# Softcap attention, gated MLP and cosine MLP on one core: both halves' attention and gated MLP first, then both cosine MLPs

## The chip, the cores and the metric

The kernel runs on one core of one Trainium2 chip. The metric is the device time of one launch in microseconds (us), taken as the median of several runs. Five engines share the core's memory (SBUF): TensorE (PE, with its weight loads PEld) does the matrix products, VectorE (DVE), ScalarE (ACT) and GpSimd (POOL) the elementwise work, SyncE (SP) issues most transfers. Each engine runs its own list of instructions strictly in order; a wait of one instruction holds up all that stand behind it.

## The reference, cut to what matters

```python
# q, k, v: (4, 12, 448, 64) float32, cap = 30
s = q @ k.T / sqrt(64);  s = cap * tanh(s / cap)
p = exp(s - max(s));     attn = p / (sum(p) + 1e-9) @ v
x = attn laid out as (1792 tokens, 768)
# gated MLP, weights float64: 768 -> 1536 -> 768
y = (1 / (1 + exp(-(x @ w_gate))) * (x @ w_val)) @ w_out
# cosine MLP, weights float64: 768 -> 2048 -> 768
h = y @ w_in;  out = (h * cos(h)) @ w_out2
```

## The kernel before, in words

The 4 batches go in two halves (hf = 0, 1) of 2 batches, 896 tokens each. A half passes through attention (L402 to L454: scores `s`, transposes `t`, products `pv` and sums `den`), the gated MLP (`pg` and `pv` by `mm3`, L461, for 12 blocks of 128 columns; then `py` for 6 blocks) and the cosine MLP. That last one takes the 16 blocks of the hidden layer in groups of 6, 5 and 5: first `ph` of each block with `hidden()` behind it (L587 to L628), then the product `po` (L549) of the group with `w_out2`, in three column parts of 256, added into `acc`.

Each product is made of three: a value is kept as a high part (a cast) and a low part (the value less the high part), and high·high, high·low and low·high are summed. So every weight and every activation is split.

The weights arrive as float64 and are taken in 70 units, 36 of the gated MLP and 34 of the cosine MLP. A unit is a raw block of 768 KB. On the first use it is converted to float32 in place of other work: ACT takes Abs and Sign (L148, L150), DVE makes four passes (L164, L166, L170, L174), SP writes the result to a buffer `kept` in device memory (L194, 384 KB). `w_split` then makes the two parts: ACT the cast (L184), POOL the difference (L185), into one of seven `wts` buffers. In the second half the unit is loaded from `kept` into an `fpool` buffer and only split. The conversions are spread by hand: `w_step`, `w_front`, `w_back` and `w_early` (L205 to L240) stand at fixed places among the matrix work and carry the pipeline one unit on.

`hidden()` takes one block: ACT copies `ph` to `h` (L624) and makes `u` (L601), DVE rounds (`n` L602, `u` L603), ACT takes the sine (L608), DVE multiplies (L609), then `n` is split into `z` (ACT L612, POOL L613). `ph` lies in one of two PSUM buffers (`psS`), so the block after next can start only when `u` of this one has been made.

The stages stand in this order (L643 to L655): attention of half 0, gated and cosine MLP of half 0 (all 70 units converted there; ten steps of half 1's attention are issued beside the last group of its cosine MLP, `BESIDE`), the rest of half 1's attention, gated and cosine MLP of half 1.

Of the kernel before, what the change touches and what calls it, by code (L numbers as in the profile page):

```python
# [27 lines left out]
def softcap_attention_gated_mlp_cos_mlp(  # L28
# [32 lines left out]
    UK = 3  # L61
    UW = 768
    RAWB = 2
    FB = 3
    LAST = 2

    BESIDE = (8, 11, 14, 15, 16, 17, 18, 19, 20)


    PVS = ((), (), (0, 1, 2, 3), ())  # L70
# [10 lines left out]
    fpool = ctx.enter_context(tc.tile_pool(name="fpool", bufs=FB))  # L81
    wts = ctx.enter_context(tc.tile_pool(name="wts", bufs=7))
    tmp = ctx.enter_context(tc.tile_pool(name="tmp", bufs=4))
    small = ctx.enter_context(tc.tile_pool(name="small", bufs=7))
    psS = ctx.enter_context(tc.tile_pool(name="psS", bufs=2, space=PSUM))
    psA = ctx.enter_context(tc.tile_pool(name="psA", bufs=4, space=PSUM))

# [19 lines left out]
                for s in range(0, nf, UK):  # L107
                    yield cols(w_out2, f"wz_{g}_{nb}_{s}", f0 + s, min(UK, nf - s), nb * NB, NB)

    first_units = list(weight_units())  # L110
    NU = len(first_units)
    units = first_units * (B // BH)
    kept = [dram.tile([P, UW], F32, tag=f"kept{i}", name=f"kept{i}") for i in range(NU)]
    SPARE = (41, NU - 8)
    raw_t, f_t, w_t = {}, {}, {}
    pos = {"load": 0, "sign": 0, "conv": 0, "keep": 0, "split": 0, "use": 0}

    def f_tile(i):
        return fpool.tile([P, UW], F32, tag="f", name=f"f{i}")

    def w_load():
        i = pos["load"]
        pos["load"] += 1
        name, src, nk, n = units[i]
        if i >= NU:
            f_t[i] = f_tile(i)
            nc.sync.dma_start(out=f_t[i][:, : nk * n], in_=kept[i - NU][:, : nk * n])
            return
        if SPARE[0] <= i < SPARE[1] and i % 3 == 0:
            t = big_tile([P, UW, 2], I32, f"{name}_raw")[:, : nk * n]  # L130
        else:
            t = wts.tile([P, UW, 2], I32, tag="w", name=f"{name}_raw")[:, : nk * n]
        nc.sync.dma_start(out=t.rearrange("p (k f) t -> p k f t", k=nk), in_=src)
        raw_t[i] = t

    def w_sign():  # L140
        i = pos["sign"]
        pos["sign"] += 1
        if i >= NU:
            return
        _, _, nk, n = units[i]
        hi = raw_t[i][..., 1].bitcast(F32)
        f_t[i] = f_tile(i)
        nc.scalar.activation(out=f_t[i][:, : nk * n], in_=hi, func=AF.Abs)  # L148
        yield
        nc.scalar.activation(out=hi, in_=hi, func=AF.Sign, bias=tiny)  # L150

    def w_conv():
        i = pos["conv"]
        pos["conv"] += 1
        if i >= NU:
            yield
            yield
            return
        _, _, nk, n = units[i]
        raw = raw_t.pop(i)  # L160
        lo, hi = raw[..., 0], raw[..., 1]
        g = f_t[i][:, : nk * n]
        gi = g.bitcast(I32)
        nc.vector.tensor_scalar(out=g, in0=g, scalar1=F64_MIN_HI, scalar2=F64_MAX_HI, op0=ALU.max, op1=ALU.min)  # L164
        yield
        nc.vector.tensor_scalar(  # L166
            out=gi, in0=gi, scalar1=4, scalar2=REBIAS, op0=ALU.logical_shift_left, op1=ALU.bitwise_xor
        )
        yield
        nc.vector.scalar_tensor_tensor(  # L170
            out=gi, in0=lo, scalar=28, in1=gi, op0=ALU.logical_shift_right, op1=ALU.bitwise_or
        )
        yield
        nc.vector.scalar_tensor_tensor(  # L174
            out=gi, in0=gi, scalar=1, in1=hi, op0=ALU.logical_shift_right, op1=ALU.bitwise_xor
        )

    def w_split():
        i = pos["split"]
        pos["split"] += 1  # L180
        name, _, nk, n = units[i]
        r = f_t.pop(i)[:, : nk * n]
        t = wts.tile([P, 2, UW], F32R, tag="w", name=f"w{i}")[:, :, : nk * n]
        nc.scalar.copy(out=t[:, 0], in_=r)  # L184
        nc.gpsimd.tensor_tensor(out=t[:, 1], in0=r, in1=t[:, 0].bitcast(F32), op=ALU.subtract)  # L185
        w_t[i] = t.rearrange("p a (k f) -> p a k f", k=nk)

    def w_keep():

        i = pos["keep"]  # L190
        pos["keep"] += 1
        if i < NU:
            _, _, nk, n = units[i]
            nc.sync.dma_start(out=kept[i][:, : nk * n], in_=f_t[i][:, : nk * n])  # L194

    def w_loads():

        spare = SPARE[0] <= pos["load"] < SPARE[1]
        while pos["load"] < min(NU, pos["conv"] + RAWB + spare) or NU <= pos["load"] < min(len(units), pos["split"] + FB):
            w_load()  # L200

    def nothing():
# [199 lines left out]
    def attention(hf):  # L402


        lo, hi = hf * BH * NP, (hf + 1) * BH * NP
        mine = pairs[lo:hi]
        n = len(mine)
        a_load(*mine[0])
        a_load(*mine[1])
        a_load(*mine[2])  # L410
        a_load_v(*mine[0])
        yield
        a_prep(*mine[0], 0)
        a_prep(*mine[0], 1)
        yield
        a_prep(*mine[1], 0)
        a_prep(*mine[1], 1)
        yield
        for i in range(n + 1):
            if i + 3 < n:  # L420
                a_load(*mine[i + 3])
            if i + 1 < n:
                a_load_v(*mine[i + 1])
            for c in range(NC):
                if i < n:
                    a_scores(*mine[i], c)
                if i and c == 0:
                    a_exp(*mine[i - 1], 1)
                if i < n and c == 2:
                    a_exp(*mine[i], 0)  # L430
                if i and c == 2:
                    a_sum(*mine[i - 1])
                if i + 2 < n and c % 2 == 0:
                    a_prep(*mine[i + 2], c // 2)
                if 1 < i < n and c == NORM:
                    a_norm(*mine[i - 2])
                if i:
                    for cc in PVS[c]:
                        a_pv(*mine[i - 1], cc)
                if 1 < i < n and c == SPLIT:  # L440
                    a_split(*mine[i - 2], nc.gpsimd)
                if i >= n - 1 and c == 3:
                    a_norm(*mine[i - 1])
                if i == n and c == 0:
                    a_split(*mine[i - 2], nc.gpsimd)
                if hf == 0 and (i, c) in UNIT_LOADS:
                    w_load()
                if hf == 0 and (i, c) in UNIT_PIECES:
                    next(pieces, None)
                yield  # L450
        if hf == 0:
            for _ in pieces:
                pass
        a_split(*mine[n - 1], nc.vector)  # L454
# [17 lines left out]
    def tmp_tile(name):  # L472
        return tmp.tile([P, BH, S], F32, tag="tmp", name=name)

    def mlp(hf, before, beside):


        x = [x_t[i] for i in range(KD)]
# [1 line left out]
        for m in range(KF):  # L480
# [30 lines left out]
            g.append(gt)  # L511
            w_step()
            w_catch()
        y = []
        for m in range(KD):
            ps = ps_tile(f"py{hf}_{m}")
            for s in range(2):
                w = w_take()
                for kk in range(KF // 2):
                    i = s * KF // 2 + kk  # L520
                    mm3(ps, w, kk, g[i], i == 0, i == KF - 1)
                w_step()
            yt = big_tile([P, 2, BH, S], F32R, f"y{hf}_{m}")
            nc.scalar.copy(out=yt[:, 0], in_=ps[:, :, :S])
            nc.vector.tensor_tensor(out=yt[:, 1], in0=ps[:, :, :S], in1=yt[:, 0].bitcast(F32), op=ALU.subtract)
            y.append(yt)
        acc = {}
        for gi, (f0, nf) in enumerate(groups):
            last = gi == len(groups) - 1
            if last:  # L530
                next(beside, None)
            z = [hidden(hf, f, y, f0 + nf - 1 - f) for f in range(f0, f0 + nf)]
            z, more = [t for t, _ in z], z[-1][1]
            zf = [t.rearrange("p a c s -> p a (c s)") for t in z]
            for nb in range(DM // NB):
                ws = [w_take() for _ in range(0, nf, UK)]
# [22 lines left out]
                for t in range(NTT):  # L559
# [21 lines left out]
                        w_back()  # L581
                    if last:
                        store(hf, t, nb, acc[nb][:, t])
                        if nb * NTT + t in BESIDE:
                            next(beside, None)

    def hidden(hf, f, y, left):  # L587

# [54 lines left out]
    with tc.manual_schedule():  # L643
        nc.vector.memset(zeros, 0.0)
        nc.vector.reciprocal(out=tanh_scale, in_=cap_sb)
        nc.vector.tensor_scalar_mul(out=tanh_scale, in0=tanh_scale, scalar1=1.0 / float(D) ** 0.5)
        nc.scalar.activation(out=guard, in_=cap_sb, func=AF.Exp, scale=-1.0)
        nc.vector.tensor_scalar_mul(out=guard, in0=guard, scalar1=1e-9 / CP)
        att = [attention(hf) for hf in range(B // BH)] + [iter(())]
        steps = 3 + (BH * NP + 1) * NC - LAST  # L650
        for hf in range(B // BH):
            for i in range(steps):
                next(att[hf])
            mlp(hf, att[hf], att[hf + 1])
            steps -= 1 + len(BESIDE)  # L655


# [33 lines left out]
```

## Time and profile before

| what | value |
|---|---|
| median of 3 runs | 1256.31 us (1250.93, 1256.31, 1257.65) |
| profiled execution, its own time | 1251.45 us |
| its span | 1249.3 us |
| PE busy | 1213.8 us, 97% |
| DVE busy | 707.7 us, 57% |
| ACT busy | 589.5 us, 47% |
| POOL busy | 451.5 us, 36% |

The span is the profiled stretch inside the execution; 2.15 us of the execution's time lie around it. The stages of the profiled execution are: up to 379.2 us attention and gated MLP of half 0; to 652.56 us its cosine MLP with ten steps of the next attention; to 754.1 us the rest of that attention; to 1007.08 us the gated MLP of half 1 (`pg` and `pv` to 917.8 us, then `py`); to 1249.3 us its cosine MLP. A busy share over the whole span is a mean over these, so the stages are read one by one.

### The profile page before, as it was taken

To read this page: it belongs to the slowest core of one execution; us is meant where nothing else is said; L and a number is where in the kernel's file an instruction comes from. 1 tells how busy PE (TensorE), PEld (TensorE's weight loads), DVE (VectorE), ACT (ScalarE), POOL (GpSimd) and SP (SyncE) were. 2 spreads that over 40 slices of the span, in tenths; PEclk is the share of its full clock that TensorE was granted. 3 is DMA by queue.
4 is the path that set the end of the run, shared out by engine and by line. 5 is a ranking of instruction groups with operands and counts; after the bars stand their busy time and mean duration, and the time that the engine had idled before them with its cause. 6 is when DMAs were issued, how large, how long until landed. Compare 5 with 4: busy or idle time off the path is not lost.

```text
span 1249.3 us, 17220 instructions
## 1 busy us (share of the span) xinstructions
PE 1213.8 (97%) x7014; PEld 1046.7 (84%) x7014; DVE 707.7 (57%) x757; ACT 589.5 (47%) x673; POOL 451.5 (36%) x234
## 2 busy tenths in 40 slices
PE   8989999999999799999899999999999999999998
PEld 4445889999999799889885559999999999999998
DVE  6998688778775975998949971111110024024252
ACT  6885554455445565646548862222221135344150
POOL 3767133223232432424426753222232224235041
PEclk9999999999999899999999999999999999999999
DMA  7522456555562463256254201211122101213013
GB/s 163 142 65 86 155 190 189 169 173 172 175 193 93 138 203 111 84 180 180 85 166 105 68 1 51 59 56 51 51 63 61 58 23 51 65 44 93 14 43 98
DMA packets 124751, 130.17 MB, mean 104 GB/s; under 512 B 49792, under 2 KB 100608, under 8 KB 124672
## 3 DMA queue, kind: packets, MB, share of 16 engines
q1 hardware_dynamic: 124384, 129.00, 34.2%
q8 instruction: 55, 0.90, 0.3%
q14 instruction: 24, 0.20, 0.1%
q10 hardware_dynamic: 288, 0.07, 0.0%
HBM read 96.80 MB, written 32.24 MB: 103 GB/s over the span
## 4 chain that ended last, share of the span: by engine, by line
PE 76%; DVE 15%; issue 4%; ACT 3%; DMA 1%; SPq 1%; POOL 1%; DVEq 0%; POOLq 0%; ACTq 0%
PE po L549 16%; PE py L461 14%; PE pv L461 13%; PE pg L461 12%; PE ph L461 11%; PE pv L369 4%; DVE f L170 3%; PE s L340 3%; DVE f L174 3%; DVE r L388 2%; PE t L319 1%; PE den L385 1%; DVE f L166 1%; ACT p L343 1%; DVE f L164 1%
## 5 line engine op out<-in xcount | busy, mean ns | idle before, releaser
L185 POOL TENSOR_TENSOR w<-f,w 128x768 fp32r<-128x768 f32 (+1 forms) x140 | 268.5, 1922 | 692.1 <-ACT w L184 614.2
L549 PE MATMUL po<-w,z 128*128 128x256 f32 x1920 | 243.4, 287 | 15.8 <-ACT w L184 5.6
L549 PEld LDWEIGHTS po<-w,z 128*128 128x128 f32 x1920 | 237.4, 195 | 19.9 <-ACT w L184 5.8
L461 PE MATMUL ph<-y,w 128*128 128x448 f32 x1152 | 235.3, 366 | 0.0
L461 PEld LDWEIGHTS ph<-y,w 128*128 128x128 f32 x1152 | 216.1, 188 | 17.9
L461 PE MATMUL pv<-x,w 128*128 128x448 f32 x864 | 181.7, 367 | 1.0 <-DVE sg L507 1.0
L461 PE MATMUL pg<-x,w 128*128 128x448 f32 x864 | 181.5, 367 | 0.0
L461 PE MATMUL py<-g,w 128*128 128x448 f32 x864 | 177.2, 367 | 0.0
L461 PEld LDWEIGHTS pv<-x,w 128*128 128x128 f32 x864 | 161.9, 188 | 17.8 <-issue 3.1
L461 PEld LDWEIGHTS pg<-x,w 128*128 128x128 f32 x864 | 162.0, 188 | 16.4 <-issue 0.7
L461 PEld LDWEIGHTS py<-g,w 128*128 128x128 f32 x864 | 162.2, 188 | 14.6
L184 ACT CAST w<-f 128x768 fp32r<-128x768 f32 (+1 forms) x140 | 112.1, 809 | 35.4 <-DVE f L174 15.5
L343 ACT ACTIVATE p<-s,tanh_scale 112x896 f32<-112x896 f32 x96 | 93.0, 1010 | 42.1 <-PE s L340 42.0
L507 DVE TENSOR_TENSOR sg<-pv,sg 128x896 f32<-128x896 f32 x24 | 26.1, 1090 | 139.7 <-PE pv L461 139.7
L602 DVE TENSOR_SCALAR n<-u 128x896 f32<-128x896 f32 (+1 forms) x38 | 25.5, 671 | 120.5 <-ACT u L601 120.5
L349 ACT ACTIVATE p<-p,cap_sb 112x1792 f32<-112x1792 f32 x48 | 86.3, 1797 | 0.1
L509 ACT CAST g<-sg 128x896 fp32r<-128x896 f32 x24 | 22.6, 942 | 132.4 <-DVE sg L507 132.4
L369 PE MATMUL pv<-p,v 112*64 112x448 f32 x384 | 77.5, 545 | 2.7 <-PE t L319 2.7
L340 PEld LDWEIGHTS s<-st 64*112 64x112 f32 x576 | 45.7, 171 | 39.7 <-ACT p L343 19.0
L388 DVE RECIPROCAL r<-den 128x448 f32<-128x448 f32 x24 | 70.8, 2950 | 8.7 <-PE den L385 8.7
L340 PE MATMUL s<-st 64*112 64x448 f32 x576 | 73.2, 380 | 1.5 <-ACT p L343 1.4
L353 POOL TENSOR_TENSOR sum<-p 112x896 f32<-112x896 f32 x24 | 56.1, 2337 | 44.1 <-ACT p L349 26.0
(75 smaller groups left out, 1176.3 us busy)
## 6 DMA issues: line engine op xcount, KB each, us to landing
kept<-f SPq DMA_DIRECT2D x64, 384.0 KB, 2.8
f<-kept SPq DMA_DIRECT2D x64, 384.0 KB, 3.1
wi_raw<-in_moe_w_in_dram SPq DMA_DIRECT2D x16, 768.0 KB, 5.1
wg_raw<-in_moe_w_gate_dram SPq DMA_DIRECT2D x12, 768.0 KB, 5.1
wv_raw<-in_moe_w_val_dram SPq DMA_DIRECT2D x12, 768.0 KB, 4.9
wo_raw<-in_moe_w_out_dram SPq DMA_DIRECT2D x12, 768.0 KB, 4.7
wz_raw<-in_moe_w_out_dram SPq DMA_DIRECT2D x12, 768.0 KB, 5.2
q<-in_q_dram SPq DMA_DIRECT2D x48, 112.0 KB, 3.1
```

What stands on the lines that cost most here:

```text
L170: nc.vector.scalar_tensor_tensor(out=gi, in0=lo, scalar=28, in1=gi, op0=ALU.logical_shift_right, op1=ALU.bitwise_or)
L174: nc.vector.scalar_tensor_tensor(out=gi, in0=gi, scalar=1, in1=hi, op0=ALU.logical_shift_right, op1=ALU.bitwise_xor)
L184: nc.scalar.copy(out=t[:, 0], in_=r)
L185: nc.gpsimd.tensor_tensor(out=t[:, 1], in0=r, in1=t[:, 0].bitcast(F32), op=ALU.subtract)
L340: nc.tensor.matmul(ps[:CP, h, :S], lhsT=st[r, ki, ks], rhs=st[r, qi], start=(n == 0), stop=(n == 2))
L343: nc.scalar.activation(out=pt[:CP, j], in_=ps[:CP, :, :S], func=AF.Tanh, scale=tanh_scale[:CP])
L349: nc.scalar.activation(out=pt[:CP], in_=pt[:CP], func=AF.Exp, scale=cap_sb[:CP])
L353: nc.gpsimd.tensor_tensor(out=s, in0=pt[:CP, 1] if half == 0 else s, in1=pt[:CP, 0], op=ALU.add)
L369: nc.tensor.matmul(pv[h * D : (h + 1) * D, :S], lhsT=tv[:, h, c, :], rhs=pt[:CP, j, h, :], start=(c == 0), stop=(c == NC - 1),)
L388: nc.vector.reciprocal(out=r[:, 0], in_=den[:, :S])
L461: nc.tensor.matmul(ps[:, c, :S], lhsT=w[:, wi, kk, :], rhs=x[:, xi, c, :], start=(first and (wi, xi) == (0, 0)), stop=(last and (wi, xi) = ...
L549: nc.tensor.matmul(pos_t[t][:, :NB], lhsT=zf[kk][:, zi, t * P : (t + 1) * P], rhs=ws[kk // UK][:, wi, kk % UK, :], start=(kk == 0 and (zi, ...
```

## The change

The stages are put in another order: attention and gated MLP of half 0, the same of half 1, then the cosine MLP of half 1, and last that of half 0. `mlp` is parted into `mlp1` and `mlp2`. Between, `y` of half 0 waits in device memory (`ykept`), unsplit; `y_again` loads and splits it during the last group of half 1's cosine MLP.

The 34 units of the cosine MLP are no longer converted where they are first used. `background()` converts them one after the other, in pieces, three to a unit: Abs and Sign of the unit with the load of the next raw block (below: s); the first two DVE passes (c1); the last two and the write to `kept` (c2). Four pieces follow each of the 12 column blocks of the second gated MLP, four stand in each block of its `py`, two follow each hidden block of the cosine MLP of half 1 and five stand among the `po` of each of its groups, until all 103 are used. Both cosine MLPs load their units from `kept`. `fpool` gets a fourth buffer, with three units loaded ahead (`AHEAD`) as before. Nine steps of half 1's attention are issued beside `py` of half 0. A `small` buffer and the spare raw buffers go, and `v` of attention is loaded some pieces later.

```diff
-    FB = 3
+    FB = 4
+    AHEAD = 3
...
-    BESIDE = (8, 11, 14, 15, 16, 17, 18, 19, 20)
+    BESIDE = ((2, 10), (3, 2), (3, 6), (4, 1), (4, 5), (4, 8), (5, 1), (5, 5), (5, 8))
+    PIECES, BESIDE_Y, PIECES_H, BESIDE_O = 4, (2, 5, 8, 11), 2, (4, 8, 12, 16, 20)
+    AGAIN = (4, 6, 8, 10, 12, 14, 16)
...
-    small = ctx.enter_context(tc.tile_pool(name="small", bufs=7))
+    small = ctx.enter_context(tc.tile_pool(name="small", bufs=6))
...
+    N1 = 2 * KF + 2 * KD
+    seq = [*range(N1)] * 2 + [*range(N1, NU)] * 2
+    units = [unit[u] for u in seq]
...
-        if SPARE[0] <= i < SPARE[1] and i % 3 == 0:
-            t = big_tile([P, UW, 2], I32, f"{name}_raw")[:, : nk * n]
-        else:
-            t = wts.tile([P, UW, 2], I32, tag="w", name=f"{name}_raw")[:, : nk * n]
+        t = wts.tile([P, UW, 2], I32, tag="w", name=f"{name}_raw")[:, : nk * n]
...
+    def background():
+        raw = {N1: raw_tile(unit[N1])}
+        yield
+        for u in range(N1, NU):
+            _, _, nk, n = unit[u]
+            g = f_tile(f"b{u}")[:, : nk * n]
+            for _ in signs(raw[u], g):
+                pass
+            if u + 1 < NU:
+                raw[u + 1] = raw_tile(unit[u + 1])
+            yield
+            c = convert(raw.pop(u), g)
+            next(c)
+            next(c)
+            yield
+            for _ in c:
+                pass
+            nc.sync.dma_start(out=kept[u][:, : nk * n], in_=g)
+            there.add(u)
+            yield
...
-        while pos["load"] < min(NU, pos["conv"] + RAWB + spare) or NU <= pos["load"] < min(len(units), pos["split"] + FB):
+        while pos["load"] < min(N1, pos["conv"] + RAWB) or N1 <= pos["load"] < min(len(units), pos["split"] + AHEAD):
...
             for c in range(NC):
+                if i + 1 < n and c == 3:
+                    a_load_v(*mine[i + 1])
...
-    def mlp(hf, before, beside):
+    def mlp1(hf, before, beside):
...
             w_step()
             w_catch()
+            if hf:
+                for _ in range(PIECES):
+                    next(beside, None)
...
                     mm3(ps, w, kk, g[i], i == 0, i == KF - 1)
+                    if hf == 0 and (m, i) in BESIDE or hf and i in BESIDE_Y:
+                        next(beside, None)
                 w_step()
+            if hf == 0:
+                yt = tmp_tile(f"y{hf}_{m}")
+                nc.scalar.copy(out=yt, in_=ps[:, :, :S])
+                nc.sync.dma_start(out=ykept[m], in_=yt)
+                continue
...
+    def y_again(y):
+        raw = {}
+        for m in range(-1, KD):
+            if m + 1 < KD:
+                raw[m + 1] = tmp_tile(f"yr{m + 1}")
+                nc.sync.dma_start(out=raw[m + 1], in_=ykept[m + 1])
+            if m >= 0:
+                t = raw.pop(m)
+                yt = big_tile([P, 2, BH, S], F32R, f"ya_{m}")
+                nc.scalar.copy(out=yt[:, 0], in_=t)
+                nc.vector.tensor_tensor(out=yt[:, 1], in0=t, in1=yt[:, 0].bitcast(F32), op=ALU.subtract)
+                y.append(yt)
+            yield
+
+    def mlp2(hf, y, others, beside):
...
-            if last:
-                next(beside, None)
-            z = [hidden(hf, f, y, f0 + nf - 1 - f) for f in range(f0, f0 + nf)]
-            z, more = [t for t, _ in z], z[-1][1]
+            z = []
+            for f in range(f0, f0 + nf):
+                t, more = hidden(hf, f, y, f0 + nf - 1 - f)
+                z.append(t)
+                for _ in range(PIECES_H):
+                    next(others, None)
...
-                        if nb * NTT + t in BESIDE:
+                        if nb * NTT + t in AGAIN:
                             next(beside, None)
+                    elif nb * NTT + t in BESIDE_O:
+                        next(others, None)
...
-        for hf in range(B // BH):
-            for i in range(steps):
-                next(att[hf])
-            mlp(hf, att[hf], att[hf + 1])
-            steps -= 1 + len(BESIDE)
+        for _ in range(steps):
+            next(att[0])
+        mlp1(0, att[0], att[1])
+        for _ in range(steps - len(BESIDE)):
+            next(att[1])
+        others = background()
+        y = mlp1(1, att[1], others)
+        y_first = []
+        mlp2(1, y, others, y_again(y_first))
+        mlp2(0, y_first, iter(()), iter(()))
```

The first place is ACT's list in the cosine MLP of half 1, from its first hidden block on; w75 and w109 are splits of weight units, z the split of the hidden value. Before:

```order
L624 COPY h1_0_8067<-ph1_0_8030 128x896 [waits PE_49]
L601 ACTIVATE u1_0_8068<-ph1_0_8030,quarter_161 128x896
L608 ACT_TABLE_LOAD
L608 ACTIVATE u1_0_8068<-u1_0_8068 128x896 [waits DVE_49]
L184 CAST w109_8077<-f109_7939 128x768 [waits DMAHW7_49,Pool_49]
L612 CAST z1_0_8070<-n1_0_8069 128x896 [waits DVE_49]
L624 COPY h1_1_8121<-ph1_1_8084 128x896 [waits PE_49]
L601 ACTIVATE u1_1_8122<-ph1_1_8084,quarter_161 128x896 [waits Activation_49]
```

And in the changed kernel, where fb60 is a buffer of `background()` and wi_12_raw the raw block:

```order
L696 COPY h1_0_5889<-ph1_0_5852 128x896 [waits PE_49]
L673 ACTIVATE u1_0_5890<-ph1_0_5852,quarter_167 128x896
L680 ACT_TABLE_LOAD
L680 ACTIVATE u1_0_5890<-u1_0_5890 128x896 [waits DVE_49]
L224 CAST w75_5899<-f75_5749 128x768 [waits DMAHW5_49,Pool_49]
L684 CAST z1_0_5892<-n1_0_5891 128x896 [waits DVE_49]
L156 ACTIVATE fb60_5909<-wi_12_raw_5822 128x768 [waits DMAHW3_49,DMAHW0_49,DVE_49]
L158 ACTIVATE wi_12_raw_5822<-wi_12_raw_5822,tiny_165 128x768 [waits Activation_49]
L696 COPY h1_1_5951<-ph1_1_5914 128x896 [waits PE_49]
L673 ACTIVATE u1_1_5952<-ph1_1_5914,quarter_167 128x896
```

Abs and Sign of fb60 (L156, L158) now stand between `z` of the first block and the copy `h` of the second, where nothing stood.

On DVE, at the same place of the changed kernel, from the multiplication of the first hidden block to c2 of the second unit:

```order
L681 TENSOR_TENSOR n1_0_5891<-h1_0_5889,u1_0_5890 128x896 [waits Activation_49]
L169 SCALAR_TENSOR_TENSOR fb59_5819<-wi_11_raw_5744,fb59_5819 128x768 [waits DMAHW4_49]
L173 SCALAR_TENSOR_TENSOR fb59_5819<-fb59_5819,wi_11_raw_5744 128x768 [waits DVE_49]
L674 TENSOR_SCALAR n1_1_5953<-u1_1_5952 128x896 [waits Activation_49]
L675 SCALAR_TENSOR_TENSOR u1_1_5952<-n1_1_5953,u1_1_5952 128x896 [waits DVE_49]
L681 TENSOR_TENSOR n1_1_5953<-h1_1_5951,u1_1_5952 128x896 [waits Activation_49]
L163 TENSOR_SCALAR fb60_5909<-fb60_5909 128x768 [waits DMAHW3_49]
L165 TENSOR_SCALAR fb60_5909<-fb60_5909 128x768 [waits DVE_49]
L169 SCALAR_TENSOR_TENSOR fb60_5909<-wi_12_raw_5822,fb60_5909 128x768 [waits DMAHW0_49,DVE_49]
L173 SCALAR_TENSOR_TENSOR fb60_5909<-fb60_5909,wi_12_raw_5822 128x768 [waits DVE_49]
```

The last two passes (L169, L173) of fb59 now stand behind the first multiplication, and all four of fb60 behind the second; the same place held the rows of `hidden()` alone.

SP's list of the changed kernel around them, where kept59 is written from fb59 and kept60 from fb60:

```order
L140 DMA f78_5902<-kept42_123 128x768 [waits DMAHW5_49,Pool_49]
L214 DMA kept59_140<-fb59_5819 128x768 [waits DMAHW3_49,DVE_49]
L147 DMA wi_13_raw_5912<-in_moe2_w_in_dram 128x6x256 [waits DMAHW4_49,PE_49]
L140 DMA f79_5964<-kept43_124 128x768 [waits DMAHW7_49,Pool_49]
L214 DMA kept60_141<-fb60_5909 128x768 [waits DMAHW6_49,DVE_49]
```

The writes to `kept` (L214), the raw loads (L147) and the loads of the next units (L140) share this list; in the second half of the kernel before it held the loads of units alone. The three units loaded ahead hold three of the four `fpool` buffers, and fb58, fb59 and fb60 are one and the same buffer.

## Rows read from the trace of the kernel before

**Rows 1.** The head of the page.

```profile
span 1249.3 us, 17220 instructions
```

**Rows 2.** Windows by stage: length, busy us (instructions) of each engine, clock, DMA share, GB/s.

```profile
379.20:652.56 273.36, 255.62 (x1661) 240.44 (x1662) 211.61 (x240) 151.91 (x195) 96.34 (x46) 0.98 0.44 136
652.56:754.10 101.54, 101.27 (x623) 54.85 (x624) 86.25 (x83) 78.24 (x67) 62.47 (x35) 1.00 0.23 58
754.10:1007.08 252.98, 252.98 (x1226) 229.75 (x1225) 31.67 (x29) 51.51 (x63) 67.29 (x36) 1.00 0.19 57
1007.08:1245.70 238.62, 238.54 (x1584) 228.90 (x1583) 73.71 (x109) 89.98 (x124) 76.97 (x41) 1.00 0.19 54
```

**Rows 3.** Chain that ended last, four of its pieces: start us, us, what.

```profile
204.30 7.29 PE pg L461 x36
...
429.89 2.00 POOL w L185
...
754.12 7.44 PE pg L461 x36
...
1097.07 36.48 PE ph L461 x180
```

**Rows 4.** Windows of three shorter stretches.

```profile
167.00:291.50 124.50, 124.00 (x613) 114.87 (x613) 98.94 (x90) 62.51 (x72) 37.73 (x18) 1.00 0.54 174
...
422.80:477.50 54.70, 47.59 (x380) 47.06 (x380) 41.58 (x46) 32.44 (x53) 16.60 (x9) 0.94 0.51 169
754.10:917.80 163.70, 163.70 (x794) 148.67 (x793) 24.03 (x22) 36.50 (x44) 43.43 (x23) 1.00 0.18 56
```

**Rows 5.** Chain of waits at 648 to 665 us, two attention pieces.

```profile
651.24 0.79 PE s L340 x6
652.03 0.53 PE t L319 x4
```

**Rows 6.** Timeline at 387 to 404 us: start, us, engine, line, operation [idle <-releaser].

```profile
388.44 0.91 ACT L148 ACTIVATE f<-wi_raw 128x768 f32<-128x768 f32 x1
...
389.38 1.01 ACT L150 ACTIVATE wi_raw<-wi_raw,tiny 128x768 f32<-128x768 f32 x1
...
390.84 0.56 DVE L166 TENSOR_SCALAR f<-f 128x768 int32<-128x768 int32 x1
...
392.69 1.09 DVE L609 TENSOR_TENSOR n<-h,u 128x896 f32<-128x896 f32 x1 [1.29 <-ACT u L608]
393.51 1.98 POOL L185 TENSOR_TENSOR w<-f,w 128x768 fp32r<-128x768 f32 x1 [18.04 <-ACT w L184]
393.69 2.61 DVE L170 SCALAR_TENSOR_TENSOR f<-wi_raw,f 128x768 int32<-128x768 int32 x1
...
396.34 2.78 DVE L174 SCALAR_TENSOR_TENSOR f<-f,wi_raw 128x768 int32<-128x768 int32 x1
...
401.80 1.09 DVE L609 TENSOR_TENSOR n<-h,u 128x896 f32<-128x896 f32 x1
```

**Rows 7.** Timeline at 1014 to 1031 us.

```profile
1014.55 0.91 ACT L624 COPY h<-ph 128x896 f32<-128x896 f32 x1 [6.53 <-PE ph L461]
...
1019.18 1.09 DVE L609 TENSOR_TENSOR n<-h,u 128x896 f32<-128x896 f32 x1 [1.02 <-ACT u L608]
1019.94 2.03 POOL L185 TENSOR_TENSOR w<-f,w 128x768 fp32r<-128x768 f32 x1 [22.34 <-ACT w L184]
...
1026.68 1.09 DVE L609 TENSOR_TENSOR n<-h,u 128x896 f32<-128x896 f32 x1 [1.02 <-ACT u L608]
```

**Rows 8.** Timeline of DVE at 226 to 232 us.

```profile
229.14 0.96 DVE L170 SCALAR_TENSOR_TENSOR f<-wv_raw,f 128x768 int32<-128x768 int32 x1
230.21 2.42 DVE L174 SCALAR_TENSOR_TENSOR f<-f,wv_raw 128x768 int32<-128x768 int32 x1
```

**Rows 9.** DMA issues of the page: KB each, us to landing.

```profile
kept<-f SPq DMA_DIRECT2D x64, 384.0 KB, 2.8
...
q<-in_q_dram SPq DMA_DIRECT2D x48, 112.0 KB, 3.1
```

More of the change, by code (lines that the diff above doesn't have):

```diff
@@ L108, in weight_units @@
                     yield cols(w_out2, f"wz_{g}_{nb}_{s}", f0 + s, min(UK, nf - s), nb * NB, NB)
-    first_units = list(weight_units())
-    NU = len(first_units)
-    units = first_units * (B // BH)
+    unit = list(weight_units())
+    NU = len(unit)
+    N1 = 2 * KF + 2 * KD
+    seq = [*range(N1)] * 2 + [*range(N1, NU)] * 2
+    units = [unit[u] for u in seq]
     kept = [dram.tile([P, UW], F32, tag=f"kept{i}", name=f"kept{i}") for i in range(NU)]
-    SPARE = (41, NU - 8)
+    ykept = [dram.tile([P, BH, S], F32, tag=f"ykept{i}", name=f"ykept{i}") for i in range(KD)]
     raw_t, f_t, w_t = {}, {}, {}
+    there = set(range(N1))
     pos = {"load": 0, "sign": 0, "conv": 0, "keep": 0, "split": 0, "use": 0}
@@ L124, in w_load, with raw_tile, signs, convert @@
         name, src, nk, n = units[i]
-        if i >= NU:
+        if i >= N1:
+            assert seq[i] in there
             f_t[i] = f_tile(i)
-            nc.sync.dma_start(out=f_t[i][:, : nk * n], in_=kept[i - NU][:, : nk * n])
+            nc.sync.dma_start(out=f_t[i][:, : nk * n], in_=kept[seq[i]][:, : nk * n])
             return
-        if SPARE[0] <= i < SPARE[1] and i % 3 == 0:
-            t = big_tile([P, UW, 2], I32, f"{name}_raw")[:, : nk * n]
-        else:
-            t = wts.tile([P, UW, 2], I32, tag="w", name=f"{name}_raw")[:, : nk * n]
+        raw_t[i] = raw_tile(unit[i])
+    def raw_tile(u):
+        name, src, nk, n = u
+        t = wts.tile([P, UW, 2], I32, tag="w", name=f"{name}_raw")[:, : nk * n]
         nc.sync.dma_start(out=t.rearrange("p (k f) t -> p k f t", k=nk), in_=src)
[L134 to L148, printed above, removed]
+        return t
+    def signs(raw, g):
+        hi = raw[..., 1].bitcast(F32)
+        nc.scalar.activation(out=g, in_=hi, func=AF.Abs)
         yield
         nc.scalar.activation(out=hi, in_=hi, func=AF.Sign, bias=tiny)
[L152 to L160, printed above, removed]
+    def convert(raw, g):
         lo, hi = raw[..., 0], raw[..., 1]
-        g = f_t[i][:, : nk * n]
         gi = g.bitcast(I32)
@@ L176, in w_conv, with w_sign @@
         )
+    def w_sign():
+        i = pos["sign"]
+        pos["sign"] += 1
+        if i >= N1:
+            return
+        _, _, nk, n = units[i]
+        f_t[i] = f_tile(i)
+        yield from signs(raw_t[i], f_t[i][:, : nk * n])
+    def w_conv():
+        i = pos["conv"]
+        pos["conv"] += 1
+        if i >= N1:
+            yield
+            yield
+            return
+        _, _, nk, n = units[i]
+        yield from convert(raw_t.pop(i), f_t[i][:, : nk * n])
+    def background():
[17 more added lines that the diff above has]
+            there.add(u)
+            yield
     def w_split():
@@ L191, in w_keep @@
         pos["keep"] += 1
-        if i < NU:
+        if i < N1:
             _, _, nk, n = units[i]
@@ L196, in w_loads @@
     def w_loads():
-        spare = SPARE[0] <= pos["load"] < SPARE[1]
-        while pos["load"] < min(NU, pos["conv"] + RAWB + spare) or NU <= pos["load"] < min(len(units), pos["split"] + FB):
+        while pos["load"] < min(N1, pos["conv"] + RAWB) or N1 <= pos["load"] < min(len(units), pos["split"] + AHEAD):
             w_load()
@@ L421, in attention @@
                 a_load(*mine[i + 3])
-            if i + 1 < n:
-                a_load_v(*mine[i + 1])
             for c in range(NC):
+                if i + 1 < n and c == 3:
+                    a_load_v(*mine[i + 1])
                 if i < n:
@@ L526, in mlp @@
             y.append(yt)
+        return y
+    def y_again(y):
[10 more added lines that the diff above has]
+                y.append(yt)
+            yield
+    def mlp2(hf, y, others, beside):
         acc = {}
@@ L648, in softcap_attention_gated_mlp_cos_mlp @@
         nc.vector.tensor_scalar_mul(out=guard, in0=guard, scalar1=1e-9 / CP)
-        att = [attention(hf) for hf in range(B // BH)] + [iter(())]
+        att = [attention(hf) for hf in range(B // BH)]
         steps = 3 + (BH * NP + 1) * NC - LAST
-        for hf in range(B // BH):
-            for i in range(steps):
-                next(att[hf])
-            mlp(hf, att[hf], att[hf + 1])
-            steps -= 1 + len(BESIDE)
+        for _ in range(steps):
[8 more added lines that the diff above has]
+        mlp2(0, y_first, iter(()), iter(()))
 _INS = ["q", "k", "v", "cap", "moe_w_gate", "moe_w_val", "moe_w_out", "moe2_w_in", "moe2_w_out"]
```

## The prediction

> **What bounds the kernel now.** I read the head of the page first: the span is 1249.3 us [rows 1], and the profiled execution took 1251.45, so 2.15 lie around the span. It is the fast end of the three runs (median 1256.31); the sum below is made against the profiled one. Then the windows by stage. TensorE is the bound nearly everywhere: in the rest of half 1's attention it is busy 101.27 of 101.54 us, in half 1's gated MLP 252.98 of 252.98, in its cosine MLP 238.54 of 238.62. The exception is the cosine MLP of half 0: 255.62 of 273.36, at a mean granted clock of 0.98 [rows 2]. That is the stage in which 34 units are converted, and half 1 does the same matrix work in 238.62. The chain of waits shows what is late there: a weight split on POOL at 429.89 ends a wait of the first `po` [rows 3], and in the window around it TensorE is busy 47.59 of 54.70 us at a granted clock of 0.94 [rows 4]. Last I read the timelines of one hidden block: with a conversion beside it the multiplications start at 392.69 and 401.80, 9.11 us apart [rows 6]; without, at 1019.18 and 1026.68, 7.50 apart [rows 7].
>
> **The change part by part.**
>
> Removed: the stage of 273.36 us [rows 2]. It holds attention of half 1 too: ten steps, of which seven are scores at 0.79 and four groups of transposes at 0.53 [rows 5], and sixteen transposes at the beginning, four such groups, 2.1: 5.5 + 2.1 + 2.1 = 9.7. Without these and the pure cosine MLP (238.6), 273.4 − 9.7 − 238.6 = 25.1 us are waits and low clock. They are what the change can win.
>
> Moved: nine of the steps now lie beside `py` of half 0 and cost TensorE 2.1 + 6 × 0.79 + 3 × 0.53 = 8.4; the tenth adds 1.3 to the rest of attention. The transposes begin some 5 us after the loads of `q`, which land in 3.1 [rows 9]; I add 1 (0 to 3).
>
> Sum without new waits, by stages [rows 2]: 379.2 up to the end of half 0's gated MLP, 8.4 + 1.3, then 101.5 + 253.0, the cosine MLP of half 1 with 238.6, and that of half 0 with the same 238.6 and the tail that follows 1245.7, 3.6. That is 1224.2, and 1225.2 with the `q` term. Storing and loading `y` costs TensorE nothing: it is copied from PSUM as before, and the seven steps of `y_again` stand in a group whose stretch of `po` is over 30 us.
>
> Added, gated MLP of half 1: 48 pieces, 16 units, in 163.70 us in which DVE is busy 24.03 and ACT 36.50 [rows 4]. In half 0 the same stage converts two units a block beside the same products, and TensorE is busy 124.00 of 124.50 [rows 4]. So the volume is hidden. The order is another matter: ACT must not write the next unit's Abs before the last unit has been written to `kept`, as both lie in the one free `fpool` buffer. In every third block the four pieces are s, c1, c2, s, a serial chain: multiplication and the POOL split beside it, 2.8 [rows 7]; Abs and Sign 1.9, two c1 passes 1.1 [rows 6]; c2 0.96 + 2.42 = 3.4 without POOL beside it [rows 8], 2.61 + 2.78 = 5.4 with it [rows 6]; landing 2.8 [rows 9]; Abs and Sign 1.9: 13.9 to 15.9 against 163.70 / 12 = 13.6 for a block. Behind it on ACT waits the next block's sigmoid. Over by 0.3 to 2.3, four times: 1 to 9; I take 2.4, since one of two PSUM buffers gives a little slack. In `py` a unit's chain of some 10 us has more room than it needs.
>
> Added, cosine MLP of half 1: here I expect the loss. With two pieces behind each hidden block, the block's own chain and the background chain run into each other on ACT. From `h` to the multiplication it takes 1019.18 − 1014.55 = 4.63 [rows 7]. The distance from one multiplication to the next is then, by what stands between:
> c2 and the next s: multiplication 1.09, c2 5.4, landing 2.8, Abs and Sign 1.9, `h` to multiplication 4.63: 15.8;
> c1 and c2: 9.11, in which c1 lay beside the sine, and 1.1 for c1 that now does not: 10.2;
> s and c1: Abs waits for the POOL split of the weights, 1021.97 − 1019.18 = 2.8, then 1.9 and 4.63: 9.3.
> The first group has 15.8 + 10.2 + 9.3 + 15.8 = 51.1 against 4 × 7.5 = 30.0. TensorE has two PSUM buffers for `ph` and stands as soon as `u` is late by more than a block: of the 21.1 some 20.5 reach it. In the second group, 10.2 + 9.3 + 15.8 = 35.3 against 22.5, and some 13 reach it. After waits of this size the granted clock falls: the window above lost 0.06 × 54.70 = 3.3 us to it [rows 4]; I add 3. Among the `po` of each group a piece s stands on ACT ahead of the copies that free PSUM, and waits for a landing of 2.8: 5.6 in both. The third group has no pieces left. Together 42.
> Ends: with c2 at 3.4 and no extras the hops are 13.8, 8.2 and 9.3, so 45.1 − 30.0 = 15 and 31.3 − 22.5 = 9: 24. With landings of 5 us and twice the clock's loss 52. At nothing it is zero, if the waits never reach TensorE.
>
> There is one more term. Matrix products ran at two speeds at the same granted clock: 36 of them took 7.29 at 204.30 and 7.44 at 754.12, and from 1097.07 on 36.48 / 5 = 7.30 again [rows 3]. The slower one held over some 300 us of half 1, 6 us in all; interruptions may end it earlier: −2.5 (−6 to +3).
>
> Sum: 1225.2 + 2.4 + 42 − 2.5 = 1267, and 2.15 around the span: 1269. Against the profiled 1251.45 that is +17.8, against the median +13.
>
> The Trainium skill (Perfetto Trace Analysis, Identifying the Most-Contended Engine) says that where the most contended engine changes over time, interleaving the stages may help; the windows agree that DVE has room in the gated MLP of half 1. By that rule alone the change would end at the second case below. The same page says that the same gap coming back on the engine that should be busy can mean too few buffers for the next tile; the forecast is a gap of that kind, and no row of the kernel before can show it.
>
> **The rivals.**
>
> 1. The conversions are hidden throughout. For it: the volume fits, DVE and ACT are idle two thirds of these stages, and in half 0 the gated MLP hid a denser conversion. Against it: the cosine MLP of half 0 did not hide its own, and there the next unit had another `fpool` buffer. Time: 1225.2 + 2 − 2.5 + 2 = 1227, to 1236 with a third of the small ends of the waits. This is the other side: the change would be faster, as long as TensorE loses less than 20 us in the cosine MLP of half 1.
>
> 2. The waits come, but at the lower ends (POOL rarely beside c2, no half clock): 1225.2 + 2.4 + 24 − 2.5 + 2.15 = 1251, no change.
>
> 3. The gated MLP of half 1 stalls as well: c2 beside POOL and landings of 5 us make the chain 18 against 13.6 in four blocks, 4 × 4.5 = 18 in place of 2.4: 1285.
>
> **How the numbers follow.** Forecast 0.55, with a range of its own of 1255 to 1282; rival 1 0.23, rival 2 0.15, rival 3 0.07. A measurement here can't tell less than about 0.5% from no change: 1250.0 to 1262.6. Slower: 0.45 of the forecast's 0.55 and rival 3: 0.52. No change: 0.10 of the forecast and 0.12 of rival 2: 0.22. Faster: rival 1 and the rest of rival 2: 0.26. The range of 1235 to 1285 leaves out most of rival 1 and half of rival 3, 0.2 together.
>
> **What would show it.** Right: in the cosine MLP of half 1, TensorE waits some 20 us before the first `po` of the first group and some 13 before that of the second, for weight splits and `u`; distances between multiplications of about 16, 10, 9 and 16; an Abs (L156) on ACT that begins when the write of the unit before it has landed; the granted clock at half after it. The cosine MLP of half 0, now last, shows none of this and lasts about 242. Wrong: that stage of half 1 lasts under 250, or the wait stands elsewhere, in the gated MLP of half 1, at the first transposes beside `py`, or at the start of the last stage for `y` loaded again.

## The result, and the profile after

The changed kernel takes 1273.04 us (median; 1271.98 to 1276.69) against 1256.58 for the kernel before beside it: 1.0145 times as long, 95% interval 1.0109 to 1.0182. The forecast was 1269. The profiled execution took 1271.98. Its span, at the head of its page, where the kernel before had 1249.3 [rows 1]:

```profile
span 1270.2 us, 17272 instructions
```

The windows by stage, columns as in [rows 2]: half 1's gated MLP and its `py`; half 1's cosine MLP whole, and its first two groups, each parted into the `ph` and the `po`.

```profile
472.30:654.30 182.00, 181.67 (x885) 163.12 (x884) 87.02 (x86) 67.61 (x77) 51.45 (x26) 1.00 0.45 145
654.30:743.90 89.60, 89.27 (x433) 81.21 (x434) 44.22 (x45) 31.25 (x39) 28.44 (x14) 1.00 0.52 163
743.90:1028.30 284.40, 251.72 (x1586) 238.66 (x1585) 127.28 (x154) 113.48 (x153) 85.06 (x44) 0.94 0.31 98
743.90:798.80 54.90, 47.50 (x218) 42.73 (x217) 31.28 (x23) 23.35 (x26) 18.03 (x8) 0.94 0.25 81
798.80:858.40 59.60, 48.67 (x380) 47.97 (x379) 19.27 (x24) 24.39 (x43) 13.43 (x7) 0.91 0.34 107
858.40:895.00 36.60, 36.60 (x183) 33.94 (x182) 20.74 (x17) 17.62 (x21) 14.96 (x7) 1.00 0.24 79
895.00:951.60 56.60, 43.70 (x316) 42.26 (x315) 25.28 (x45) 16.87 (x24) 13.97 (x8) 0.85 0.33 105
```

And the last stage, the cosine MLP of half 0, with the tail behind it:

```profile
1028.30:1266.25 237.95, 237.95 (x1586) 229.11 (x1584) 75.30 (x111) 87.47 (x122) 78.61 (x42) 1.00 0.20 59
1266.25:1270.20 3.95, 0.00 (x1) 0.00 (x0) 0.42 (x1) 0.00 (x0) 0.00 (x0) 0.86 0.19 57
```

Read the first number (length) against the second (TensorE busy), and the clock near the end of the row. The gated MLP is full in spite of 87 us of DVE work. The cosine MLP of half 1 takes 284.40 where half 0's takes 237.95. Of these 46 us 32.7 are idle (284.40 − 251.72), and 13 are longer matrix work at a mean granted clock of 0.94 (251.72 against 238.54 in [rows 2]). Nearly all of it lies in the first group and in the `po` of the second. The stage of 273.36 us with its waits [rows 2] is gone, as forecast.

What TensorE waited for between 480 and 1010 us (total, times, longest), its first three rows:

```profile
PE po L619 <- ACT w L224: 7.8, 1, 7.8
PE ph L500 <- ACT u L673: 7.4, 2, 4.7
PE po L619 <- ACT z L684: 5.5, 2, 3.3
```

These are what stands last in the chain of a hidden block: `u`, `z`, and the weight split in the same list on ACT. Call the stretch from one hidden block's multiplication on DVE to the next one's a hop. The chain of waits over the first hop shows who is before them (start, us, what); its last row, further down in the same view, is the fifth multiplication:

```profile
756.08 1.09 DVE n L681
757.17 2.53 DVE fb L169
759.73 2.77 DVE fb L173
762.51 2.76 DMA kept<-fb
...
765.38 0.91 ACT fb L156
...
766.31 0.97 ACT wi_raw L158
767.28 0.79 ACT h L696
768.07 0.92 ACT u L673
...
806.98 1.10 DVE n L681
```

The pieces follow one another without a gap: the multiplication, the two passes of c2, the landing of the write, Abs and Sign of the next unit, and only then `h` and `u` of the next block. The timeline: POOL beside c2 in the first hop, then the second hop and the starts of the multiplications after it:

```profile
756.85 2.02 POOL L225 TENSOR_TENSOR w<-f,w 128x768 fp32r<-128x768 f32 x1 [13.69 <-ACT w L224]
...
758.83 2.84 POOL L685 TENSOR_TENSOR z<-n,z 128x896 fp32r<-128x896 f32 x1
...
765.38 0.90 ACT L156 ACTIVATE fb<-wi_raw 128x768 f32<-128x768 f32 x1 [7.23 <-DMA kept<-fb]
...
771.78 1.09 DVE L681 TENSOR_TENSOR n<-h,u 128x896 f32<-128x896 f32 x1 [1.02 <-ACT u L680]
772.55 2.04 POOL L225 TENSOR_TENSOR w<-f,w 128x768 fp32r<-128x768 f32 x1 [10.88 <-ACT w L224]
772.79 2.21 DVE L163 TENSOR_SCALAR fb<-fb 128x768 f32<-128x768 f32 x1
...
774.55 2.44 POOL L685 TENSOR_TENSOR z<-n,z 128x896 fp32r<-128x896 f32 x1
...
775.04 2.36 DVE L165 TENSOR_SCALAR fb<-fb 128x768 int32<-128x768 int32 x1
777.43 0.96 DVE L169 SCALAR_TENSOR_TENSOR fb<-wi_raw,fb 128x768 int32<-128x768 int32 x1
778.43 0.96 DVE L173 SCALAR_TENSOR_TENSOR fb<-fb,wi_raw 128x768 int32<-128x768 int32 x1
...
782.07 1.09 DVE L681 TENSOR_TENSOR n<-h,u 128x896 f32<-128x896 f32 x1 [1.02 <-ACT u L680]
...
791.30 1.09 DVE L681 TENSOR_TENSOR n<-h,u 128x896 f32<-128x896 f32 x1 [1.01 <-ACT u L680]
```

ACT stood idle 7.23 us before Abs, released by the write to `kept`. With 756.08 and 806.98 from the chain, the multiplications start 15.70, 10.29, 9.23 and 15.68 us apart, where [rows 7] had 7.50.

### The profile page after: what moved, and what is told of

It is laid out like the page before. It is cut to its first block, busy times and chain, and to the rows that moved or that the text cites. A ratio compares the mean times of both kernels' runs of the same rounds, so it can differ in the third digit from the quotient of the medians.

```text
span 1270.2 us, 17272 instructions
## 1 busy us (share of the span) xinstructions
PE 1220.0 (96%) x7014; PEld 1051.7 (83%) x7014; DVE 696.4 (55%) x757; ACT 593.5 (47%) x678; POOL 449.9 (35%) x234
## 4 chain that ended last, share of the span: by engine, by line
PE 72%; DVE 13%; ACT 6%; issue 4%; DMA 3%; POOL 1%; SPq 1%; DVEq 0%; ACTq 0%; POOLq 0%
PE po L619 16%; PE ph L500 13%; PE py L500 12%; PE pv L500 11%; PE pg L500 10%; PE pv L408 4%; PE s L379 3%; DMA kept<-fb 2%; DVE r L427 1%; PE t L358 1%; DVE fb L169 1%; DVE fb L173 1%; ACT p L382 1%; DVE f L169 1%; PE den L424 1%
## 5 line engine op out<-in xcount | busy, mean ns | idle before, releaser
L225 POOL TENSOR_TENSOR w<-f,w 128x768 fp32r<-128x768 f32 (+1 forms) x140 | 271.3, 1943 | 704.0 <-ACT w L224 572.9
L500 PE MATMUL ph<-y,w 128*128 128x448 f32 x576 | 121.0, 372 | 7.4 <-ACT u L673 7.4
L500 PEld LDWEIGHTS ph<-y,w 128*128 128x128 f32 x576 | 110.2, 192 | 17.4 <-ACT u L673 8.2
L500 PE MATMUL ph<-ya,w 128*128 128x448 f32 x576 | 117.2, 365 | 0.0
L500 PEld LDWEIGHTS ph<-ya,w 128*128 128x128 f32 x576 | 108.0, 188 | 8.5
L163 DVE TENSOR_SCALAR fb<-fb 128x768 f32<-128x768 f32 (+1 forms) x34 | 30.0, 882 | 82.6 <-ACT fb L156 82.6
```

Source lines behind the costliest of these rows:

```text
L500: nc.tensor.matmul(ps[:, c, :S], lhsT=w[:, wi, kk, :], rhs=x[:, xi, c, :], start=(first and (wi, xi) == (0, 0)), stop=(last and (wi, xi) = ...
```

## The experiments

**Two buffers in place of one.** Two units are loaded ahead, so `background()` has two of the four buffers.

```diff
-    AHEAD = 3
+    AHEAD = 2
```

> One number is changed: two units are loaded ahead of the split in place of three, so that background() has two of the four fpool buffers. Nothing else moves. Theory (one free buffer: Abs waits for the write of the unit before): Abs of the next unit then waits only for a POOL split, so the distances between multiplications in the first group of half 1's cosine MLP become 9.3, 10.2, 9.3, 9.3 = 38.1 in place of 15.7, 10.3, 9.2, 15.7, that is some 8 us of wait in the first group, 6 in the second, 3 of half clock: the stage 256 in place of 284.4, the kernel 1244 (1236 to 1252). Rival (the added work of ACT and DVE beside hidden blocks delays them, whatever the buffers): as the changed kernel, 1265 to 1276.

Measured: 1249.07, ratio to before 0.9969 (0.9939 to 0.9999). The Abs that had waited 7.23 us for a write now waits for a POOL split, as its row on ACT says; under it, in a fence of their own, the first four multiplications on DVE, and then the whole stage:

```profile
760.49 0.92 ACT L156 ACTIVATE fb<-wi_raw 128x768 f32<-128x768 f32 x1 [1.63 <-POOL w L225]
```

```profile
756.79 1.09 DVE L681 TENSOR_TENSOR n<-h,u 128x896 f32<-128x896 f32 x1 [1.02 <-ACT u L680]
...
766.95 1.09 DVE L681 TENSOR_TENSOR n<-h,u 128x896 f32<-128x896 f32 x1 [1.02 <-ACT u L680]
...
777.24 1.09 DVE L681 TENSOR_TENSOR n<-h,u 128x896 f32<-128x896 f32 x1 [1.02 <-ACT u L680]
...
785.90 1.09 DVE L681 TENSOR_TENSOR n<-h,u 128x896 f32<-128x896 f32 x1 [1.02 <-ACT u L680]
```

```profile
744.60:1007.30 262.70, 247.99 (x1586) 235.79 (x1585) 130.47 (x155) 113.61 (x153) 85.75 (x44) 0.96 0.33 103
```

10.16, 10.29 and 8.66 apart, and 22 us less in the stage than the 284.40 of the changed kernel. The same instructions at the same places cost less once the buffer is there, so the rival, that they cost as much whatever the buffers, falls. But it falls for half of the loss only: 262.70 is still 25 us over the 237.95 of half 0's cosine MLP, and the hops are still longer than 7.50. That half is the time that the pieces themselves take beside a hidden block; how much of it is POOL holding up DVE, no run separates. The theory had left 17 of it. TensorE's idle time is as it put it, 14.7 (8 and 6 expected); the longer matrix work at a lower clock is 9.5 us (247.99 against 238.54 in [rows 2]) where 3 was expected, and that makes the 5 us by which the kernel missed 1244.

**No conversions.**

```diff
-            assert seq[i] in there
...
-            nc.sync.dma_start(out=f_t[i][:, : nk * n], in_=kept[seq[i]][:, : nk * n])
+            nc.sync.dma_start(out=f_t[i][:, : nk * n], in_=kept[seq[i] % N1][:, : nk * n])
...
-        others = background()
+        others = iter(())
```

> The changed kernel without background(): the cosine MLP's weights are not converted, written or loaded raw; its units are loaded from the kept units of the gated MLP instead. Theory (all of the loss comes from the conversions): half 1's cosine MLP takes 239 as that of half 0 does, the span is 1225 and the time 1227 (1222 to 1232). Rival (the new order, storing and loading y, or the shared queue cost something by themselves): over 1238.

Measured: 1231.48, in one run. Both cosine MLPs, half 1's first:

```profile
747.30:988.00 240.70, 239.30 (x1586) 229.22 (x1585) 78.08 (x112) 97.69 (x133) 81.58 (x44) 1.00 0.23 70
988.00:1225.90 237.90, 237.90 (x1585) 229.09 (x1584) 75.01 (x111) 87.55 (x122) 78.62 (x42) 1.00 0.20 59
```

So the new order, with `y` stored and loaded, costs some 3 us at most (240.70 against 237.90, taken up below), and all the rest of the loss hangs on the conversions.

**The same shortage in another stage.**

```diff
-    PIECES, BESIDE_Y, PIECES_H, BESIDE_O = 4, (2, 5, 8, 11), 2, (4, 8, 12, 16, 20)
+    PIECES, BESIDE_Y, PIECES_H, BESIDE_O = 6, (2, 5, 8, 11), 0, (4, 8, 12, 16, 20)
```

> All background pieces but a few leave the hidden blocks: six in place of four behind each block of half 1's gated MLP, none beside hidden blocks; still one free fpool buffer. Theory (one free buffer makes a unit a serial chain): two units a block need 18 to 22 us (Abs and Sign 1.9, c1 1.1, c2 3.4 to 5.4, landing 2.8, twice) against 14.6 for a block, so the waits come back in the gated MLP: 12 x 4 to 8 = 45 to 95 us there, none in half 1's cosine MLP: 1270 to 1320. Rival (the gated MLP hides two units a block whatever the buffers, as it does in half 0): 1230.

Measured: 1284.99, in one run. The gated MLP of half 1, and ACT's longest sum of waits in it (total, times, longest):

```profile
472.70:703.10 230.40, 196.01 (x884) 173.79 (x884) 115.64 (x114) 77.32 (x88) 52.37 (x26) 0.93 0.47 144
```

```profile
ACT fb L156 <- DMA kept<-fb: 97.2, 17, 7.7
```

34 us idle and a granted clock of 0.93, in a stage that in half 0 was full with two units a block [rows 4]. 17 of the 22 Abs between 484 and 704 us wait for a write. The cosine MLP of half 1 is clean but for 2 us of idle time. With the same pieces and two buffers:

> As the run before, with two units loaded ahead, so two fpool buffers for background(). Theory: units overlap, the gated MLP hides two of them a block as it does in half 0, and the cosine MLP of half 1 runs as in the kernel before: 1232 (1226 to 1242). Rival (the place decides, not the buffer): like the run before within 10 us.

Measured: 1232.31, ratio 0.9847 (0.9809 to 0.9885). Gated and cosine MLP of half 1:

```profile
472.70:660.50 187.80, 183.48 (x884) 162.63 (x884) 116.62 (x116) 80.47 (x92) 51.80 (x26) 1.00 0.52 171
...
748.40:989.00 240.60, 239.14 (x1586) 229.49 (x1585) 91.44 (x123) 100.71 (x137) 82.20 (x44) 1.00 0.25 76
```

53 us between the two runs by one buffer. With one buffer the place of the pieces decided where the wait for the write fell, in the cosine MLP or here; with two, the gated MLP kept 4 us of idle time of 34.

**The write taken out.** `background()` doesn't store; the load shown with the run without conversions stands in for it.

```diff
-            nc.sync.dma_start(out=kept[u][:, : nk * n], in_=g)
-            there.add(u)
```

> The changed kernel without the writes of background() to kept: units are converted as before, but not stored, and the cosine MLPs load kept units of the gated MLP in their place. Still one free buffer; the next Abs now waits for the last DVE pass alone. Theory: c2 and the next s give 1.09 + 5.4 + 1.9 + 4.63 = 13.0 in place of 15.7, so distances 13.0, 10.3, 9.2, 13.0: 5.5 less in the first group, 2.7 in the second, and up to 5.6 less among the po: 1273 - 11 to 14 and some half clock: 1259 (1253 to 1264). Rival (the write is off the path, the DVE passes alone hold Abs): 1270 and over.

Measured: 1264.15, in one run, 9 less than with the write and just past the expected stretch. The kernel before took 1252.44 beside this run and 1256.58 beside the changed kernel, so some 4 us of the 9 may not be the write; the stage is the surer measure, 276.8 us (743.4 to 1020.2) in place of 284.4. The first four multiplications on DVE:

```profile
755.72 1.09 DVE L678 TENSOR_TENSOR n<-h,u 128x896 f32<-128x896 f32 x1 [1.02 <-ACT u L677]
...
768.60 1.09 DVE L678 TENSOR_TENSOR n<-h,u 128x896 f32<-128x896 f32 x1 [1.02 <-ACT u L677]
...
778.88 1.09 DVE L678 TENSOR_TENSOR n<-h,u 128x896 f32<-128x896 f32 x1 [1.02 <-ACT u L677]
...
788.10 1.09 DVE L678 TENSOR_TENSOR n<-h,u 128x896 f32<-128x896 f32 x1 [1.01 <-ACT u L677]
```

12.88, 10.28 and 9.22: the hop is shorter by 2.8, the landing [rows 9], and otherwise the same. So the landing is a small part, some 8 of the stage's 46 us; the passes of c2 and the order of ACT's list hold the rest of the hop.

**The pieces dealt otherwise, one buffer kept.**

```diff
-    PIECES, BESIDE_Y, PIECES_H, BESIDE_O = 4, (2, 5, 8, 11), 2, (4, 8, 12, 16, 20)
+    PIECES, BESIDE_Y, PIECES_H = 4, (2, 5, 8, 11), (1, 2, 1, 2, 1, 2)
+    BESIDE_O = ((1, 6, 7, 8, 13, 14, 15, 19, 20), (3, 4, 5, 12, 13, 14), ())
...
-                for _ in range(PIECES_H):
+                for _ in range(PIECES_H[f - f0]):
...
-                    elif nb * NTT + t in BESIDE_O:
+                    elif nb * NTT + t in BESIDE_O[gi]:
```

> The changed kernel with one free buffer as it is, and the pieces dealt out in another way: one, two, one, two pieces behind hidden blocks in place of two each, so that c2 stands alone and the next s comes a block later, when the write has landed; the pieces left over go among the po, nine and six in place of five and five, with s well behind c2. Theory (the loss is the coincidence of c2 and the next s on ACT's list): distances 9.2, 9.3, 9.2, 9.3 = 37 against 30, so 7 of wait in the first group, 5 in the second, 0 to 6 among the po and 3 to 6 of half clock: 1247 (1241 to 1255), as with two free buffers. Rival (one buffer costs its landing wherever the pieces stand): 1262 to 1275.

Measured: 1246.87, ratio 0.9951 (0.9925 to 0.9976). Multiplications, and the stage:

```profile
756.14 1.09 DVE L682 TENSOR_TENSOR n<-h,u 128x896 f32<-128x896 f32 x1 [1.02 <-ACT u L681]
...
765.24 1.09 DVE L682 TENSOR_TENSOR n<-h,u 128x896 f32<-128x896 f32 x1 [1.02 <-ACT u L681]
...
774.52 1.09 DVE L682 TENSOR_TENSOR n<-h,u 128x896 f32<-128x896 f32 x1 [1.02 <-ACT u L681]
...
783.60 1.09 DVE L682 TENSOR_TENSOR n<-h,u 128x896 f32<-128x896 f32 x1 [1.02 <-ACT u L681]
```

```profile
743.90:1003.70 259.80, 247.60 (x1586) 236.18 (x1584) 126.57 (x156) 113.61 (x153) 87.23 (x44) 0.97 0.34 108
```

9.10, 9.28 and 9.08: the long hop is gone, and one buffer does as well as two when the next s does not stand right behind c2. The deal also takes 6 of the 22 pieces away from the hidden blocks of the first two groups, and how much of the 25 us won in the stage is due to that, the run doesn't show. 22 us over half 0's cosine MLP stay here too.

**The subtraction of `y_again` on POOL.**

```diff
-                nc.vector.tensor_tensor(out=yt[:, 1], in0=t, in1=yt[:, 0].bitcast(F32), op=ALU.subtract)
+                nc.gpsimd.tensor_tensor(out=yt[:, 1], in0=t, in1=yt[:, 0].bitcast(F32), op=ALU.subtract)
```

> As gate6_a2, and the subtraction in y_again runs on POOL in place of DVE. In all runs with y_again the po of the last group of half 1's cosine MLP took 2.5 to 3 us longer than in the kernel before, without conversions too. Theory: the subtraction (1.09) stands on DVE ahead of the additions into acc, which free PSUM for the next po, and waits there for ACT and the load of y; on POOL it holds up no addition: that group back to 38.0 from 40.7, 1230 in all. Rival (the queue of loads and stores on SP, fuller there, makes it late): still 40.5.

Measured: 1233.17 in its one run, not less. But the last group's `po`, on DVE and then on POOL:

```profile
948.30:989.00 40.70, 39.24 (x318) 38.21 (x317) 18.27 (x34) 14.04 (x20) 11.62 (x8) 1.00 0.56 166
```

```profile
951.20:989.20 38.00, 38.00 (x317) 37.88 (x316) 13.51 (x29) 13.95 (x20) 21.50 (x13) 1.00 0.63 189
```

The 2.7 us went, as expected. What took them back lies in half 0, where no line differs: its gated MLP ran from 120.2 to 294.8 us in place of 120.3 to 292.7, with TensorE busy 173.40 us in place of 171.42 for 842 products.

**The fastest version.** The kernel just shown, with another deal of the pieces:

```diff
-    PIECES, BESIDE_Y, PIECES_H, BESIDE_O = 6, (2, 5, 8, 11), 0, (4, 8, 12, 16, 20)
+    PIECES, BESIDE_Y, PIECES_H, BESIDE_O = 5, (1, 3, 5, 7, 9, 11), 0, (4, 8, 12, 16, 20)
```

> For the fastest version: two units loaded ahead, five pieces behind each block of half 1's gated MLP and six in each block of its py, none beside hidden blocks, the subtraction of y_again on POOL. Theory: six pieces a block kept TensorE idle for some 4 us of that stage (183.48 busy of 187.80); five should leave under 2: 1228 (1223 to 1233). Rival: six pieces within a py block crowd ACT and lose it again there: 1232 to 1237.

Measured: 1228.65, ratio 0.9801 (0.9770 to 0.9831). Its gated MLP of half 1, `py` and cosine MLP:

```profile
484.15:658.50 174.35, 173.31 (x843) 157.75 (x842) 104.49 (x98) 71.70 (x82) 47.85 (x23) 1.00 0.50 162
658.50:746.00 87.50, 87.50 (x433) 81.10 (x433) 54.61 (x61) 38.90 (x47) 25.09 (x13) 1.00 0.73 232
746.00:983.80 237.80, 237.80 (x1585) 229.12 (x1584) 86.61 (x118) 100.77 (x137) 91.48 (x49) 1.00 0.26 79
```

TensorE is idle for 1 us in the three together.

## Why the prediction was right

*The terms outside the wait.* `py` of half 0 with nine steps took 96.2 us (292.3 to 388.5) against 87.6 before (291.7 to 379.2), 8.7 more where 8.4 were forecast; the 1 us for `q` didn't come. The last stage with its tail took 241.9, forecast 242.2.

*The wait chain.* This step carried the forecast, and it held: in its place, in its mechanism and in the size of its hops. Hops of 15.8, 10.2, 9.3 and 15.8 were forecast; 15.70, 10.29, 9.23 and 15.68 were measured. The second came out right with another working: c1 was put at 1.1 us and c2 at 5.4, and it was c1 that met POOL (4.57 for its two passes) and c2 that did not (1.92). The stage lost 46 us where 42 were forecast. The two parts were not right each for itself: I had 39 of waiting and 3 of low clock, and it was 33 and 13. Of the waiting in the second group, 9.5 us lay before the bulk of its `po`, not 13, and the 5 us among the `po` of both groups, put at 5.6, came otherwise: an s that waited for a weight split on POOL held up the copies in one group, and its c1 the additions in the other, and neither waited for the landing of a write. The clock term was mis-sized: I took the loss of one window before the change for the whole stage, where three of its windows above lie under full clock, down to 0.85. That the sum came within 4 us of the measurement is in part luck, as the waits were put 6 too high, the low clock 10 too low and the gated MLP 2.4 too high.

*Gated MLP of half 1.* Forecast +2.4; it took 182.0 and lost nothing. The working had an error: I divided 163.70 by twelve blocks, but the window has 794 matmuls [rows 4], and a block has 72, so it held eleven. A block is 14.8 us, not 13.6, and the chain of 13.9 to 15.9 about fits.

*`y_again`* was put at nothing and cost some 2.7, as the run with the subtraction on POOL shows; on DVE the subtraction stood ahead of the additions that free PSUM.

*Matrix products at two speeds.* −2.5 forecast; the gated MLP of half 1 and the last stage together came out 1.6 shorter than before, but this term can't be told from chance.

*The rivals.* The first (all hidden) was not this kernel, but it was right on the volume: with a second buffer and no pieces beside hidden blocks the kernel runs at its 1227 to 1236. It is also the case to which interleaving alone would lead; the prediction calls that the second case, but in its list it is the first. So the new order of the stages can gain 1.5 to 2%; the change lost it, and more, by one buffer and by pieces beside the hidden blocks, each worth about half of the stage's 46 us. The second rival's lower ends were wrong since c2 had POOL beside it in each of the long hops; the third did not come.

## What to carry to other kernels

Background work dealt in pieces onto engines that run in order must be checked as a chain, piece behind piece: where one piece ends in a transfer and the next one needs its buffer, keep them a block apart or give a second buffer. Either removed about half of the loss here; the other half went only when the pieces left the stage whose own chain was tight. That an engine is idle half of a stage says the volume fits, not the order. Before a time is divided by a count, take the count from the same row.

## What the runs showed of the hardware

A pass of the conversion on DVE that met a running POOL instruction ended after it, in each of the rows shown, whichever pass it was: in the timeline above the first pass of c1 took 2.21 and the second 2.36, beside POOL subtractions of 2.04 and 2.44, and 0.56 alone [rows 6]; each ended 0.41 us after the POOL instruction. The two passes of c2 behind them took 0.96 each. In the hop before it was c2 that paid: 2.53 and 2.77 in the chain, beside 2.02 and 2.84 on POOL. The Trainium skill (SBUF — State Buffer, Who interferes with whom) says that where a VectorE instruction needs the ports that it shares with GpSimd, whichever of the two issues first has them for its whole instruction and the other is blocked fully; these rows agree.

TensorE's waits in half 1's cosine MLP, 33 us in all and up to 7.8 us each, brought 13 us of longer matrix work with them. The granted clock was 0.50, the lower of its two levels, from 788.5 to 793.5 us behind a wait of 4.66 us and from 807.7 to 812 behind one of 7.77; behind the wait of 2.73 us that ended at 769 it stayed at 1.00. This cost shrank less than the waits did: with two buffers, 14.7 us of waits came with 9.5 us of longer work, and with the pieces dealt otherwise 12.2 with 9.1.

The kernel before spread from 1246.77 to 1259.66 over 17 runs, and half 0's gated MLP, from its first `pv` to its first `py` the same matrix products in every run here, took 172.4 us in some profiles (before, after, two buffers with six pieces) and 174.7 in others (the same with the subtraction on POOL, the fastest version) at a granted clock of 1.00. What sets that speed stays open.
